# Last chunk of a Fourier mixing and gated feed-forward kernel: output product straight from h, in output rows

## The chip, the core and the metric

The kernel runs on one core of a Trainium2 chip. Five engines work side by side, each through its own list of instructions in order: TensorE (PE; its weight loads are shown as PEld), VectorE (DVE), ScalarE (ACT), GpSimd (POOL) and SyncE (SP), which here only issues transfers. ACT issues some transfers too. The metric is the time of one execution in microseconds (us) on the device.

## The reference

```python
batch, seq, dim = (8, 3008, 256)          # x, float32
X = np.fft.fft(x, axis=1)
X = np.fft.fft(X, axis=2)
x = X.real.astype(np.float32).reshape(24064, 256)
gate = 1.0 / (1.0 + np.exp(-(x @ w_gate)))   # w_gate, w_val: (256, 1536)
val = x @ w_val
out = (gate * val @ w_out).astype(np.float32)   # w_out: (1536, 256)
```

The three weight matrices come as float64; the kernel gets them as pairs of 32-bit words and converts them to float32 itself.

## The kernel before

**Staging.** The transform along the sequence uses the symmetry of cosine and sine: frequency k and its mirror image S − k come from the same two sums, kept for each batch element in tiles `pk` and `qk`, with the model dimension on partitions. The transform along the model dimension is multiplied into the gate and value weights once, at the start (`G1`, `G2`). So the feed-forward part begins with products of `G1` with `pk` and of `G2` with `qk`; their sum and their difference are the values of a frequency and of its mirror image.

**The main loop.** A batch element has 1505 frequencies, cut into six chunks: five of 252 columns and one of 246. Each chunk runs over 12 blocks `f` of 128 hidden features. That gives 8 x 6 x 12 = 576 iterations `i` of one loop (`count`), which is written out in order by hand (line 854): every engine's instructions stand in the order of the Python calls, and semaphores are put in from the tiles' use. An iteration has, in this order:

- `front_a(i)`: two products `pf<-pk,G` on PE into an accumulator bank (PSUM).
- `gate_a(i-1)`: ACT's sigmoid `h<-pf` (L627), and DVE's `z<-ae,pf` (L632), the other side's values.
- `part(i)`: ACT copies twice the `pk` part to `ae` (L608). The next products into that bank wait for it.
- `seed(i+1)`: two ACT instructions (L592) fill the next bank with one frequency's row.
- `gate_b(i-1)`: DVE's product L644, ACT's sigmoid L645 `z<-z`, DVE's product L646 `h<-z`; then POOL's sums `sf` (L650).
- `back`: five output products `po` for the group of features that was finished some iterations earlier.
- `front_b(i)`: two products `pf<-qk,G`.
- some entries of the list `later`, and whatever the table `side` holds for this iteration, at its end.

**The output product.** `h` holds, for 128 hidden features on partitions, both sides of the chunk: 2n columns. The 12 blocks go in four groups of three (`g`). Instead of 18 products of 128x128 blocks with a third of the columns each, a group needs 15, of sums of `h` blocks (`H_SUMS`, made on POOL) with sums of output-weight blocks (`wf`, made once at the start by `forms`). They accumulate over the four groups in five banks `po0` to `po4`. `back(p, part)` makes five products of group `p` in each of three iterations; for the last group of a chunk it also copies the banks to a tile `c` (ACT or DVE, L674). `finish` then needs 20 sums (`C_SUMS`, `C_LAST`; DVE, L697), four 32x32 block transposes (`flip`, L707), since the products lie with output features on partitions, and 16 stores (`store`, L716 and L720). For all chunks but the last these are put into `later`, two or three to an iteration (three in the last eight), so the chunk before last has its sums, transposes and stores inside the last chunk's iterations. For the last chunk they run at once; there POOL takes some of the sums, ACT issues half of the stores, and the last bank is read where it is.

**Tiles with one slot.** The pool `op` has a single slot for the tile `os` that takes the transposes; a new `os` waits for the transfers that read the one before. The pool `xp` has a single slot `x4` for the input of a batch element; the last one is read at iteration 472.

**Weights.** `weight_load` loads 256x256 float64 words (512 KB) on SP; `weight_parts` are two ACT instructions (L295, L296), `weight_join` three on DVE (L305, L306, L308) and an integer addition on POOL (L310). Before the change all weights pass through these in the first ten iterations or ahead of the loop, and only the sums of output weights in `wf` are kept.

Of the kernel before, what the change touches and what calls it, by code (L numbers as in the profile page):

```python
# [7 lines left out]
F32 = mybir.dt.float32  # L8
I32 = mybir.dt.int32
U32 = mybir.dt.uint32  # L10
AF = mybir.ActivationFunctionType
ALU = mybir.AluOpType
# [55 lines left out]
PLACE = (0, 1, 2, 5, 3, 4, 6, 7, 8, 9, 10, 11, 14, 13, 12)  # L68


C_SUMS = (((3, 3, 1, 0), 0), ((3, 3, 0, 1), 0), ((8, 1, 8, 0), 0), ((1, 6, 2, 0), 1), ((0, 0, 10, 1), 0),
          ((11, 0, 11, 0), 0), ((9, 9, 8, 0), 1), ((11, 11, 5, 0), 0), ((4, 4, 0, 1), 1),
          ((6, 11, 6, 0), 0), ((4, 4, 1, 0), 1), ((9, 13, 9, 1), 0), ((10, 14, 8, 1), 0), ((9, 9, 2, 0), 0),
          ((12, 9, 12, 0), 0), ((12, 12, 11, 1), 0), ((13, 13, 6, 1), 0),
          ((7, 7, 10, 0), 1), ((5, 5, 7, 1), 1))
C_LAST = (14, 9, 14, 0)
OUT = (3, 12)
HUGE = float((2 ** 24 - 1 - 2 ** 20) * 2.0 ** -7)
# [3 lines left out]
def kernel(  # L82
# [10 lines left out]
    nc = tc.nc  # L93
    B, _, _, _, D = xf.shape
    F = moe_w_gate.shape[1]
    P = 128
    S = out.shape[0] // B
    M = S // 2
    NK = M + 1
    NE = (M // 2) // 2 + 1  # L100
    NO = (M // 2) // 2
    NFT = F // P
    NPR = NFT // 2
    NG = NFT // 3
    CH = 252
    NB = 1 + max(b // 3 for b in PLACE)
# [26 lines left out]
    def mm(o, l, r, start, stop):  # L133
        nc.tensor.matmul(o, l, r, start=start, stop=stop, skip_group_check=True)  # L134
# [155 lines left out]
    def weight_parts(j):  # L290

        if j in RAW:
            raw, ws = RAW[j], WS[j]
            lo, hi = raw[:, :, :, 0], raw[:, :, :, 1]
            nc.scalar.activation(ws, hi.bitcast(F32), AF.Abs)  # L295
            nc.scalar.activation(lo, lo.bitcast(U32), AF.Copy, scale=2.0 ** -29)  # L296

    def weight_join(j):
        if j not in RAW:
            return  # L300
        raw, ws = RAW.pop(j), WS[j]
        lo, hi = raw[:, :, :, 0], raw[:, :, :, 1]
        wi = ws.bitcast(I32)
        ts = nc.vector.tensor_scalar
        ts(out=ws, in0=ws, scalar1=2.0 ** -15, scalar2=HUGE, op0=ALU.max, op1=ALU.min)  # L305
        ts(out=wi, in0=wi, scalar1=3, scalar2=0x3FFFFFF8, op0=ALU.logical_shift_left,  # L306
           op1=ALU.bitwise_and)
        nc.vector.scalar_tensor_tensor(out=wi, in0=hi, scalar=-(2 ** 30), in1=wi,  # L308
                                       op0=ALU.bitwise_and, op1=ALU.bitwise_or)
        nc.gpsimd.tensor_tensor(wi, wi, lo, op=ALU.add)  # L310

    WO, parts_ = {}, []

    def weight_use(j, other=None):
        w, c = jobs[j]
# [299 lines left out]
    def front_b(i):  # L615
        (_, qk, *_), ks, _, _, fs = cut(i)
        for g in range(2):
            mm(PF[i][:, g], G2[:, g, fs], qk[:, ks], False, True)
# [20 lines left out]
    def gate_b(i):  # L639

        n = cut(i)[2]
        p, fh = i // 3, i % 3
        z, h = Z.pop(i), H[p]
        nc.vector.tensor_tensor(h[:, fh, 0:n], h[:, fh, 0:n], PF.pop(i)[:, 1], op=ALU.mult)  # L644
        nc.scalar.activation(z[:, 0], z[:, 0], AF.Sigmoid)  # L645
        nc.vector.tensor_tensor(h[:, fh, n:], z[:, 0], z[:, 1], op=ALU.mult)  # L646
        if fh == 1:
            SF[p] = sp.tile([P, 8, 2 * CH // 3], F32, name="sf", tag="sf")
        for dst, a, b, op in H_SUMS.get(fh, ()):
            nc.gpsimd.tensor_tensor(block(p, dst), block(p, a), block(p, b),  # L650
                                    op=(ALU.subtract, ALU.add)[op])

    PO = []
    later = []
    C = {}

    def back(p, part):

        b, c, g = groups[p]
        n = chunks[c][1]  # L660
        R = 2 * n // 3
        last = p == len(groups) - 1
        if part == 0 and g == 0:
            PO[:] = [pso.tile([P, 2 * WC], F32, name=f"po{t}", tag=f"po{t}") for t in range(NB)]
        for at_, (hb, wb) in list(enumerate(PRODUCTS))[part * 5 : part * 5 + 5]:
            t, j = divmod(PLACE[at_], 3)
            mm(PO[t][:, j * R : (j + 1) * R], wf[:, g, wb], block(p, hb), g == 0 and at_ % 3 == 0,
               g == NG - 1)
            if g == NG - 1 and at_ % 3 == 2:
                if t == 0:  # L670
                    C[0] = cp.tile([P, 10 * WC], F32, name="c", tag="c")
                    nc.gpsimd.memset(C[0][:, 15 * R : 15 * R + 40], 0.0)
                if not (last and t == NB - 1):
                    (nc.vector.tensor_copy if t == 1 or t == 3 and not last else nc.scalar.copy)(  # L674
                        C[0][:, 3 * t * R : 3 * (t + 1) * R], PO[t][:, 0 : 3 * R])
        if part == 2:
            del H[p], SF[p]
            if g == NG - 1:
                finish(b, c, last)

    def finish(b, c, last):
        k0, n = chunks[c]
        R = 2 * n // 3
        more = k0 + n > NK
        nb = -(-n // TB)
        t = C.pop(0)
        queues = (nc.sync, nc.scalar) if last else (nc.sync,)
        os_ = []

        new = set()  # L690

        def sum_(dst, a, b, op, engine=nc.vector):

            there = lambda i: last and i >= 3 * (NB - 1) and i not in new
            v = [PO[NB - 1][:, (i - 3 * NB + 3) * R : (i - 3 * NB + 4) * R] if there(i) else
                 t[:, i * R : (i + 1) * R] for i in (a, b)]
            engine.tensor_tensor(t[:, dst * R : (dst + 1) * R], *v, op=(ALU.subtract, ALU.add)[op])  # L697
            new.add(dst)

        def flip(s, h):  # L700
            if not os_:

                full = (sp.tile([P, 8 * (2 * CH // 3)], F32, name="os", tag="sf") if last else
                        op.tile([P, NK + 1], F32, name="os", tag="os"))
                os_.append(full[:, 0 : 4 * WC].rearrange("p (s b h j) -> p s b h j", s=2, h=2, j=TB))
            c0 = OUT[h] * R + (n + more if s else 0)
            nc.vector.transpose(os_[0][:, s, 0:nb, h, :], t[:, c0 : c0 + nb * TB])  # L707

        def store(s):
            m, r0 = (min(n, M - k0), b * S + k0) if s == 0 else (  # L710
                n - (k0 == 0) - more, b * S + S - k0 - n + 1 + more)
            full = m // TB
            for a in range(4):
                ps = slice(a * TB, (a + 1) * TB)
                cs = slice(a * 2 * TB, (a + 1) * 2 * TB)
                queues[a % len(queues)].dma_start(  # L716
                    out=out[r0 : r0 + full * TB, cs].rearrange("(b t) d -> t b d", t=TB),
                    in_=os_[0][ps, s, 0:full].rearrange("p b h j -> p b (h j)"))
                if m > full * TB:
                    queues[a % len(queues)].dma_start(out=out[r0 + full * TB : r0 + m, cs],  # L720
                                      in_=os_[0][a * TB : a * TB + m - full * TB, s, full].rearrange(
                                          "p h j -> p (h j)"))

        def add(f):
            if last:
                f()
            else:
                later.append(f)
        for x, e in C_SUMS:
            if x[0] == 7:  # L730
                add(lambda: flip(0, 0))
                add(lambda: (flip(0, 1), store(0)))
            add(lambda x=x, e=e: sum_(*x, engine=(nc.vector, nc.gpsimd)[last and e]))
        add(lambda: sum_(*C_LAST))
        add(lambda: flip(1, 1))
        add(lambda: (flip(1, 0), store(1)))


# [61 lines left out]
    def at(i, *fs):  # L800
        side.setdefault(i, []).extend(fs)
# [29 lines left out]
    for b in range(B - 1):  # L831
# [17 lines left out]
        if b < B - 2:  # L849
            at(g0 + 1, lambda b=b: load_x(b + 2))  # L850
            for i, f in zip(calm(s0 if b else 3 * i0), mirror_x(b + 2)):
                at(i, f)

    for i in range(count):
        front_a(i)
        if N1 <= i < NFT:
            part(i)
        if i:
            gate_a(i - 1)
        if not N1 <= i < NFT:  # L860
            part(i)
        if i0 <= i + 1 < count:
            seed(i + 1)
        if i:
            gate_b(i - 1)
        todo = pre.pop(i, []) + use.pop(i, [])
        for f in [parts_.pop(0)] + todo if parts_ else todo + [lambda: parts_ and parts_.pop(0)()]:
            f()
        if i >= 5:
            back((i - 5) // 3, (i - 5) % 3)  # L870
        front_b(i)
        n = 3 if i >= count - 8 else 2 + i % 2
        for f in later[0:n]:
            f()
        del later[0:n]
        for f in side.pop(i, []):
            f()
    gate_a(count - 1)
    gate_b(count - 1)
    for f in later:  # L880
        f()
    for i in range(count, count + 5):
        back((i - 5) // 3, (i - 5) % 3)


# [47 lines left out]
```

## Time and profile before

| what | us |
| --- | --- |
| median of 3 runs | 1958.39 |
| lowest, highest run | 1955.29, 1959.18 |
| profiled execution: span from first to last instruction | 1957.5 |
| PE busy | 1915.8 (98%) |
| DVE, ACT, POOL busy | 1600.5, 1334.1, 1645.6 |
| granted TensorE clock, mean | 0.995 of full speed |

The page gives no other time of the profiled execution than its span; what the device spends around the first and the last instruction isn't in it. The span lies inside the range of the three runs.

How to read the rows: in the groups, "out<-in" are the program's tile names with partitions x elements; "xN" is the number of instructions; then busy time, mean duration, and the idle time of the engine ahead of them with what ended it. A float32 product appears as two weight loads and two matrix multiplications, so five products are ten records. In rows in order of time the first number is the start from the span's beginning, the second the duration, and the bracket the idle time ahead and its releaser. PE's rows end when the result is written, so successive ones overlap; the chain of waits counts each from where the one before it ended.

### The profile page before, as it was taken

Reading aid. Unit: us, or ns where it says so; the run is one execution under the profiler, and the core shown is the slowest. Engines: PE = TensorE matmul, PEld = TensorE weight load, DVE = VectorE, ACT = ScalarE, POOL = GpSimd, SP = SyncE. Lnnn points to the kernel's source line nnn. Section 1 sums busy time; section 2 is a strip of 40 time slices with the busy share of each in tenths; the row PEclk is TensorE's granted clock in tenths of the full one; section 3 lists DMA queues with packets and bytes.
Section 4 is the critical chain, followed back from the end, with each engine's and each line's share of the span. In section 5 each row is a group of like instructions: output and inputs, shape, how many; then the busy total and the mean of one; then the engine's idle time right before and its main releaser. Section 6 shows DMA issues by size and latency. Waiting matters only on the chain.

```text
span 1957.5 us, 34550 instructions
## 1 busy us (share of the span) xinstructions
PE 1915.8 (98%) x11252; PEld 1788.6 (91%) x11252; DVE 1600.5 (82%) x3271; ACT 1334.1 (68%) x3122; POOL 1645.6 (84%) x2853
## 2 busy tenths in 40 slices
PE   5999999999999999999999999999999999999997
PEld 3889899999999999999999999999999999999997
DVE  6888797898888878888878888788888887777777
ACT  2567667666777767776777767777677776777775
POOL 3779898997999978997889978998799996777776
PEclk9999999999999999999999999999999999999999
DMA  8352423212012120222012021211210110011011
GB/s 269 90 134 23 99 47 111 46 19 84 17 47 53 21 78 15 55 51 73 21 23 77 20 79 23 44 53 20 82 19 14 20 22 14 14 21 20 14 19 28
DMA packets 169746, 96.78 MB, mean 49 GB/s; under 512 B 133858, under 2 KB 161636, under 8 KB 167020
## 3 DMA queue, kind: packets, MB, share of 16 engines
q1 hardware_dynamic: 167596, 94.02, 20.2%
q8 instruction: 90, 1.47, 0.3%
q10 hardware_dynamic: 1940, 0.56, 0.2%
q14 instruction: 88, 0.72, 0.1%
q0 software_dynamic: 32, 0.00, 0.0%
HBM read 69.83 MB, written 46.71 MB: 60 GB/s over the span
## 4 chain that ended last, share of the span: by engine, by line
PE 90%; POOL 4%; DVE 3%; DMA 2%; ACT 1%; issue 0%; ACTq 0%; DVEq 0%; SPq 0%; POOLq 0%
PE pf L134 47%; PE po L134 39%; PE ev L134 2%; POOL sf L650 2%; DVE c L697 1%; DMA st<-in_stab_dram 1%; PE od L134 1%; PE ps L134 1%; DMA ge<-G 1%; DVE h L646 1%; DVE z L632 0%; ACT z L645 0%; POOL x L401 0%; DMA raw<-in_moe_w_gate_dram 0%; POOL x L417 0%
## 5 line engine op out<-in xcount | busy, mean ns | idle before, releaser
L650 POOL TENSOR_TENSOR sf<-h 128x168 f32<-128x168 f32 (+1 forms) x960 | 551.0, 593 | 196.9 <-DVE h L646 196.8
L650 POOL TENSOR_TENSOR sf<-h,sf 128x168 f32<-128x168 f32 (+1 forms) x1152 | 663.4, 595 | 46.7 <-DVE h L646 46.7
L134 PE MATMUL pf<-qk,G 128*128 128x252 f32 (+1 forms) x2304 | 583.0, 376 | 7.8 <-ACT ae L608 5.7
L134 PE MATMUL pf<-pk,G 128*128 128x252 f32 (+1 forms) x2304 | 583.7, 376 | 0.0
L646 DVE TENSOR_TENSOR h<-z 128x252 f32<-128x252 f32 (+1 forms) x576 | 316.5, 549 | 296.8 <-ACT z L645 294.9
L592 ACT ACTIVATE pf<-ek,ge 128x252 f32<-128x252 f32 (+1 forms) x1128 | 531.7, 471 | 18.4
L134 PE MATMUL po<-sf,wf 128*128 128x168 f32 (+1 forms) x3072 | 530.8, 306 | 0.2
L697 DVE TENSOR_TENSOR c<-c 128x168 f32<-128x168 f32 (+1 forms) x949 | 512.4, 571 | 5.5 <-ACT c L674 0.3
L134 PEld LDWEIGHTS pf<-pk,G 128*128 128x128 f32 x2304 | 436.3, 190 | 53.5 <-issue 1.6
L608 ACT ACTIVATE ae<-pf 128x504 f32<-128x504 f32 (+1 forms) x569 | 335.3, 589 | 216.1 <-PE pf L134 214.7
L134 PEld LDWEIGHTS po<-sf,wf 128*128 128x128 f32 x3072 | 473.3, 190 | 9.2 <-POOL sf L650 0.9
L134 PE MATMUL po<-h,wf 128*128 128x168 f32 (+1 forms) x2688 | 476.3, 306 | 0.0
L134 PEld LDWEIGHTS po<-h,wf 128*128 128x128 f32 x2688 | 428.1, 190 | 16.8
L134 PEld LDWEIGHTS pf<-qk,G 128*128 128x128 f32 x2304 | 409.8, 190 | 35.5 <-ACT ae L608 7.4
L632 DVE TENSOR_TENSOR z<-ae,pf 128x504 f32<-128x504 f32 (+1 forms) x569 | 377.7, 664 | 15.6 <-ACT h L627 15.2
L645 ACT ACTIVATE z<-z 128x252 f32<-128x252 f32 (+1 forms) x576 | 232.6, 404 | 161.5 <-DVE z L632 139.9
L627 ACT ACTIVATE h<-pf 128x252 f32<-128x252 f32 (+1 forms) x576 | 217.0, 377 | 125.9 <-PE pf L134 113.4
L644 DVE TENSOR_TENSOR h<-h,pf 128x252 f32<-128x252 f32 (+1 forms) x576 | 232.2, 403 | 0.0
L650 POOL TENSOR_TENSOR sf<-sf 128x168 f32<-128x168 f32 (+1 forms) x192 | 111.5, 581 | 15.1
L650 POOL TENSOR_TENSOR sf<-sf,h 128x168 f32<-128x168 f32 (+1 forms) x192 | 109.3, 569 | 0.0
L134 PE MATMUL ev<-st,x 63*128 63x189 f32 (+3 forms) x372 | 73.3, 347 | 11.5 <-DVE x L398 9.0
L674 ACT COPY c<-po 128x504 f32<-128x504 f32 (+1 forms) x144 | 80.2, 557 | 3.1 <-PE po L134 3.1
(138 smaller groups left out, 880.1 us busy)
## 6 DMA issues: line engine op xcount, KB each, us to landing
x<-xr SPq DMA_DIRECT2D x14, 1536.0 KB
out_dram<-os SPq DMA_DIRECT2D x380, 56.0 KB
xr<-in_xf_dram SPq DMA_DIRECT2D x14, 768.0 KB
xr<-in_xf_dram SPq DMA_DIRECT2D x35, 256.0 KB
ek<-ed SPq DMA_DIRECT2D x39, 126.0 KB
out_dram<-os SPq DMA_DIRECT2D x288, 7.0 KB
st<-in_stab_dram SPq DMA_DIRECT2D x4, 1111.9 KB
x<-in_xf_dram SPq DMA_DIRECT2D x2, 1512.0 KB
```

What stands on the lines that cost most here:

```text
L134: nc.tensor.matmul(o, l, r, start=start, stop=stop, skip_group_check=True)
L592: nc.scalar.activation(PF[i][:, g], EK[i // NFT], AF.Copy, scale=ge[:, g, f : f + 1])
L608: nc.scalar.activation(AP[i], PF[i], AF.Copy, scale=2.0)
L627: nc.scalar.activation(H[p][:, fh, 0:n], PF[i][:, 0], AF.Sigmoid)
L632: nc.vector.tensor_tensor(z[:, :, ::-1], AP.pop(i), PF[i], op=ALU.subtract)
L644: nc.vector.tensor_tensor(h[:, fh, 0:n], h[:, fh, 0:n], PF.pop(i)[:, 1], op=ALU.mult)
L645: nc.scalar.activation(z[:, 0], z[:, 0], AF.Sigmoid)
L646: nc.vector.tensor_tensor(h[:, fh, n:], z[:, 0], z[:, 1], op=ALU.mult)
L650: nc.gpsimd.tensor_tensor(block(p, dst), block(p, a), block(p, b), op=(ALU.subtract, ALU.add)[op])
L674: (nc.vector.tensor_copy if t == 1 or t == 3 and not last else nc.scalar.copy)(C[0][:, 3 * t * R : 3 * (t + 1) * R], PO[t][:, 0 : 3 * R])
L697: engine.tensor_tensor(t[:, dst * R : (dst + 1) * R], *v, op=(ALU.subtract, ALU.add)[op])
```

## The change

The last chunk (`p >= P_LAST`, the last four groups) doesn't use the sums:

- `gate_b` ends after `h` there: no `sf`, no POOL sums.
- Instead of `back`, a new function `straight(f)` multiplies one feature block of `h`, as the stationary operand, by 128 rows of the plain output weights. Its result has tokens on partitions, 256 output features in the columns, as the output has them. There are four row tiles (128, 116, 128 and 117 tokens: two for each side), two to a bank, so four products of 256 columns for each `f`, 48 in all. After the last `f` each tile is copied to `od` (DVE for tiles 0 and 2, ACT for 1 and 3) and stored by one transfer (SP and ACT). `od` is taken from the slot of `os`.
- The table `STRAIGHT` says which `f` is made in which of the last seven iterations; three are left for after the loop.
- The plain output weights aren't there any more, so `late_weights` loads them again, in six loads, into the slot `x4`: at iteration `count - 48 + 4c`, with `weight_parts` two iterations later and `weight_join` three iterations later, at the end of the iteration.
- `C_SUMS` loses its engine marks, and `back` and `finish` their cases for the last chunk.

```diff
+    def late_weights(c):
+        if not WL:
+            WL[0] = xp.tile([P, 24, WC], F32, name="wl", tag="x4")
+        ws = WL[0][:, 2 * c : 2 * c + 2]
+        src = moe_w_out[2 * c * P : 2 * (c + 1) * P, :].rearrange("(c p) f -> p c f", p=P)
...
+            r = 12 + c % 3 * 4
+            raw = WL[0][:, r : r + 4].rearrange("p a n -> p (a n)")
+            RAW[j] = raw.bitcast(I32).rearrange("p (c f w) -> p c f w", c=2, w=2)
+            nc.sync.dma_start(out=RAW[j].rearrange("p c f w -> p c (f w)"), in_=src.bitcast(I32))
...
         nc.vector.tensor_tensor(h[:, fh, n:], z[:, 0], z[:, 1], op=ALU.mult)
+        if p >= P_LAST:
+            return
...
+    def straight(f):
+        if not PD:
+            PD.extend(pso.tile([P, 2 * WC], F32, name=f"pd{t}", tag=f"po{t}") for t in range(2))
+            OD.append(op.tile([P, NK + 1], F32, name="od", tag="os")[:, 0 : 4 * WC].rearrange(
+                "p (t d) -> p t d", d=WC))
+        h = H[P_LAST + f // 3]
+        for t, (c0, m, row) in enumerate(tiles()):
+            o = PD[t // 2][0:m, t % 2 * WC : (t % 2 + 1) * WC]
+            mm(o, h[:, f % 3, c0 : c0 + m], WL[0][:, f], f == 0 and t % 2 == 0, f == NFT - 1)
+            if f == NFT - 1:
+                (nc.scalar.copy if t % 2 else nc.vector.tensor_copy)(OD[0][0:m, t], o)
+                (nc.scalar if t % 2 else nc.sync).dma_start(out=out[row : row + m, :], in_=OD[0][0:m, t])
...
+    for c in range(NPR):
+        i = count - 4 * i0 + 4 * c
+        at(i, lambda c=c: late_weights(c))
+        at(i + 2, lambda c=c: weight_parts(len(jobs) + c))
+        at(i + 3, lambda c=c: weight_join(len(jobs) + c))
+    STRAIGHT = {count - 7: (0, 1), count - 6: (2, 3), count - 5: (4,), count - 4: (5,), count - 3: (6,),
+                count - 2: (7,), count - 1: (8,), count: (9, 10, 11)}
...
-        if i >= 5:
+        if 5 <= i < 3 * P_LAST + 5:
             back((i - 5) // 3, (i - 5) % 3)
+        for f in STRAIGHT.pop(i, ()):
+            straight(f)
...
     for f in later:
         f()
-    for i in range(count, count + 5):
-        back((i - 5) // 3, (i - 5) % 3)
+    for f in STRAIGHT.pop(count):
+        straight(f)
```

## The prediction

> **What bounds the kernel now.** I read the page's first part, the waits of the last 150 us, the instructions in order of time for one ordinary iteration, for a stalled one and for the end, and then the rows of the weight conversion.
>
> ```profile
> PE 1915.8 (98%) x11252; PEld 1788.6 (91%) x11252; DVE 1600.5 (82%) x3271; ACT 1334.1 (68%) x3122; POOL 1645.6 (84%) x2853
> ```
>
> TensorE is the bound. In the waits from 1800 to 1935 us nobody makes PE wait: DVE waits for ACT, ACT for PE.
>
> ```profile
> POOL sf L650 <- DVE h L646: 32.1, 30, 2.0
> DVE h L646 <- ACT z L645: 29.6, 43, 1.3
> ACT ae L608 <- PE pf L134: 19.5, 44, 0.5
> ```
>
> Near there an iteration recurs every 3.125 us (252 columns), 3.05 us in the last chunk (246). One of them, in order of time (start, us, engine, what):
>
> ```profile
> 1815.50 1.85 DVE L697 TENSOR_TENSOR c<-c 128x168 f32<-128x168 f32 x3
> 1816.37 0.59 ACT L608 ACTIVATE ae<-pf 128x504 f32<-128x504 f32 x1 [0.47 <-PE pf L134]
> 1817.27 0.67 DVE L632 TENSOR_TENSOR z<-ae,pf 128x504 f32<-128x504 f32 x1
> 1817.46 0.76 PEld L134 LDWEIGHTS pf<-qk,G 128*128 128x128 f32 x4
> 1817.96 0.41 ACT L645 ACTIVATE z<-z 128x252 f32<-128x252 f32 x1
> ```
>
> PE needs ae, which ends 0.50 us ahead of its next pf products. ACT's L645 waits for DVE's z and stands ahead of the next ae, so a late DVE can reach PE. At 373 us it did:
>
> ```profile
> 372.89 0.59 ACT L608 ACTIVATE ae<-pf 128x504 f32<-128x504 f32 x1 [0.47 <-PE pf L134]
> 373.39 3.30 DVE L697 TENSOR_TENSOR c<-c 128x168 f32<-128x168 f32 x3
> 376.61 0.67 DVE L632 TENSOR_TENSOR z<-ae,pf 128x504 f32<-128x504 f32 x1
> 378.53 1.12 PE L134 MATMUL pf<-qk,G 128*128 128x252 f32 x4 [1.12 <-ACT ae L608]
> ```
>
> Three sums took 3.30 us beside large POOL work, z began 3.72 us after ae began, and that iteration of PE lasted 4.515 us, 1.4 too long. So z may begin 2.3 us after ae for nothing. Ordinarily DVE is free for its sums 0.87 us before ae (1815.50 against 1816.37): up to 3.17 us of work on DVE there is free.
>
> The end:
>
> ```profile
> 1939.94 0.77 DVE L707 STREAM_TRANSPOSE os<-c 128x256 f32<-128x256 f32 x2
> 1944.36 0.42 SPq L720 DMA_DIRECT2D out_dram<-os  x1
> 1944.62 2.11 PE L134 MATMUL po<-sf,wf 128*128 128x164 f32 x14
> 1946.53 2.25 DVE L697 TENSOR_TENSOR c<-c 128x164 f32<-128x164 f32 x4 [0.30 <-ACT c L674]
> 1951.38 0.77 DVE L707 STREAM_TRANSPOSE os<-c 128x256 f32<-128x256 f32 x2
> 1955.16 0.28 SPq L720 DMA_DIRECT2D out_dram<-os  x1
> ```
>
> PE ends at 1946.73; sums, transposes and stores take 10.8 us more to the span's 1957.5. The last pf product ends at F = 1939.77 by the chain of waits; from F to the end are 17.7 us.
>
> **The change, part by part.** Removed in the last chunk: 52 POOL sums of 0.54 to 0.6 us (beside PE, worth nothing on the path except through DVE's freedom), five po copies, all sums and transposes after PE, 16 small stores on SP and ACT.
>
> *PE.* Sixty products of 164 columns become 48 of 256. The chain has five of 164 in 1.39 us and 984 columns of pf in 1.66: both 1.69 ns a column. So 0.278 us a product before, 0.433 after; 16.7 us become 20.8, plus 4.1. By the order of the instructions two iterations get eight products each (3.46 for 1.39: plus 2.07 twice) and five get four (1.73: plus 0.34), so F moves by 5.85. After it 12 products stay (5.2) where 25 were (6.96). Nothing waits for the new products' weights or for h, which is three iterations old; only the last three f follow F closely, and h of the last (2.4 us after F in the old trace, 1939.77 to 1942.15) is ready before the 3.46 us of the two ahead of it are done.
>
> *The last row tiles.* In the changed order the copy of tile 0 from the accumulator (DVE) waits for eight DMA semaphores: `od` has the slot of the chunk before's `os`, whose stores must have landed. The second matmul into each bank waits for that bank's first copy, because the copy is written ahead of it. Tile 0 is multiplied at F + 9 x 0.433 = 3.9. The old stores end with the issue at 1944.36, F + 4.6, and land 1.45 later: F + 6.0. In the new run DVE makes the transposes some 0.8 us earlier against F (a longer iteration, no POOL sums), but SP still issues 16 stores at about 0.43 each, so I take half, F + 5.55. Then: DVE copy 0.43 (0.67 for 492 columns, L674, with 0.16 fixed); hand-over 0.06; matmul of tile 1 to its result 0.74 (0.58 for 164 columns at 1922.27, plus 92 x 1.69 ns); tile 2 0.43; its copy 0.48; tile 3 with hand-over 0.80; ACT copy 0.42; issue 0.05; landing 1.9 (1.2 to 1.8 for the last old stores by the trace's semaphore records; more bytes here); 1.1 from the last landing to the end, as before. F + 12.0. With F 5.85 later that is 17.8 against 17.7: plus 0.1. Bounds: without the store wait tile 0's copy starts at F + 4.1, 1.45 earlier (minus 1.3 in all); a landing like that of the ek load, 2.9, gives plus 1.1. I stay at the step's own sum, since the eight semaphores stand in the order.
>
> One rule concerns the stores. The Trainium skill, DMA: Bandwidth & Descriptors, in Why a DMA increments its semaphore by 16 and not by 1, says a copy from SP or ACT is spread over the largest number of engines up to 16 that divides its rows: 4 engines for the 116 rows of tile 1, 13 for the 117 of tile 3. No run here has such a store; if tile 1's became the last to land, the end would move beyond this sum.
>
> *Late weights.* Six times, four iterations apart from iteration 528: a 512 KB load on SP; two iterations later two ACT passes; one later three DVE passes and a POOL add.
>
> ```profile
> L295 ACT ACTIVATE wx<-wx x8: 664/670/679, 56.2 to 97.0; 128x512 f32<-128x512 f32 x8
> L305 DVE TENSOR_SCALAR wx<-wx x8: 412/716/764, 61.2 to 102.6; 128x512 f32<-128x512 f32 x8
> L306 DVE TENSOR_SCALAR wx<-wx x8: 427/646/1401, 61.6 to 103.4; 128x512 int32<-128x512 int32 x8
> L308 DVE SCALAR_TENSOR_TENSOR wx<-wx x8: 693/910/1664, 62.1 to 104.1; 128x512 int32<-128x512 int32 x8
> ```
>
> Loads: the wx loads landed 3.8 us after issue, the use is 6.2 after: hidden. On SP each stands ahead of eight stores and the next ek load, needed eight iterations later: hidden, unless SP is held over 20 us.
>
> ACT: 2 x 0.67 = 1.34 us behind L645 and ahead of the next ae. In the ordinary iteration ACT idles 0.5 and 0.47 there, so ae is 0.4 late; it has 0.5 less a 0.06 hand-over: nothing. In iterations 530 and 542 a 0.56 copy of po stands there too: ae is 0.9 late, PE loses some 0.35, twice: 0.7.
>
> DVE: 1.54 us by the shortest rows, 2.27 by the medians, 4.1 by the longest; the long ones lay beside POOL work. After the chunk's other DVE work: iterations 531, 543 have a copy (0.68), 535, 547 three sums (1.16, POOL mostly idle there), 539, 551 two transposes and a sum (1.4) beside POOL's sums. With 2.27 the three are 2.95, 3.43 and 3.67 against 3.17; in 535 and 547, where POOL idles, I take 1.54: 2.7. So only 539 and 551 stall, 0.5 each: 1.0. Lower end nothing (1.54 everywhere: 2.2, 2.7, 2.9); upper end, 4.1 six times: 1.6, 2.1 and 2.3, twice, 12 us. I take the median, as POOL is busy about three quarters of this stretch.
>
> POOL: 1.29 us more (L310) in 12.5, which adds a tenth to 77% busy; its sums are read two iterations later: hidden.
>
> A rule speaks against the change here. The row first: c sums take 0.33 us alone and about 0.6 beside POOL's, so POOL costs each about half of one of its own instructions. The Trainium skill, SBUF — State Buffer, SBUF: two separate sides, says the port pair of VectorE and GpSimd is an exclusive lock, and the loser is blocked for a whole instruction. By the rule each of the three passes waits one POOL sum and the join takes 3.3 us, and the whole change costs 8 us instead of 2.
>
> *Sum.* 4.1 of PE is inside the tail's plus 0.1; ACT 0.7; DVE 1.0: plus 1.8 us. The profiled execution is its span of 1957.5 us, 0.9 under the median of 1958.39 and inside the three runs; I add to the median: **1960.2 us**. About 0.2%, 3.9 us, is what a measurement of this kernel can tell from no change.
>
> **The rivals.** *Slower: the joins starve the gates.* If POOL stretches the three DVE passes everywhere, z comes late six times and PE stops behind L645. Halfway between the median and the longest rows, at 3.2 us, the excess over 3.17 is 0.7, 1.2 and 1.4, twice: 6.6, and with 0.8 from the rest 7.4: 1965.8. It leaves the band of no change where the join's mean passes 2.6 us. For it: 373 us, and L306 and L308 at twice their shortest time. Against it: those lie beside 128x512 POOL folds, which this stretch no longer has.
>
> *A small gain.* The store wait does not bind and the conversions hide: minus 1.3, 1957.1. For it: ACT and DVE idle a fifth of the stretch. Against it: SP's 0.43 us issues are regular.
>
> *Faster by over 0.2%.* Even without bank waits (12 products 5.2, result 0.3, copy 0.42, issue 0.05, landing 1.9, end 1.1: F + 9.0) the tail saves 2.9 us, so this needs an error in the PE step too.
>
> **How the numbers follow.** Forecast 0.46, small gain 0.08, starving 0.40, faster 0.06. Same is 0.54. The range goes from a gain of about 2 us, 1956.4, to past the starving case, 1966.5; the forecast's own is 1958 to 1962.3.
>
> **What would show it.** Right: pd products 0.43 us apart, PE gaps only near iterations 530, 539, 542, 551, of 0.3 to 0.5 us; F 5.85 plus those gaps later; the first od copy released by a DMA, some 1.5 us after tile 0's product; 12 us from F to the end. Wrong: PE gaps of 1 us at every join; wl landing after its use; a last store that lands 3 us after issue; pd products over 0.45 us.

## The result

The changed kernel takes 1962.97 us (median of 22 runs, 1959.35 to 1967.47), the kernel before 1956.63 in the same comparison (22 runs, 1953.96 to 1964.57): a ratio of 1.0031, 95% interval 1.0024 to 1.0038. It is about 6.1 us slower, more than the 0.2% that can be told from no change. The forecast was a loss of 1.8 us, within that band. 1962.97 lies in the whole range that was given and the direction holds, but it is above the forecast's own 1958 to 1962.3, and the loss is over three times the forecast: by that band of 0.2% the outcome is the slower one, which had a chance of 0.40 against the forecast's 0.46.

The profiled execution of the changed kernel took 1961.92 us, its span is 1960.1. Against the span of before that is only 2.6 us more, since the profiled run of before lost time at its start: the main loop's iteration 1 began at 58.02 us there and at 54.23 here, while the other profiles of this study have 53.3 to 55.4. From that iteration to the end the changed kernel needs 6.4 us more, which fits the ratio.

**Where they are.** I took the start of the first `pf` product of every iteration from the trace. Iterations are 3.125 us apart where nothing stalls.

| stretch | before | predicted | after |
| --- | --- | --- | --- |
| iterations 531 to 556, the six conversions: stalls | 0 | 1.7 | 6.1 |
| start of iteration 564 to that of 575: the new products in the loop | 33.74 | 39.20 | 39.20 |
| start of iteration 575 to the end | 20.93 | 15.57 | 15.95 |

The second row has the growth of 5.46 us that belongs to iterations before 575 (569 and 570 with 2.06 each, 571 to 574 with 0.335); the rest of the 5.85 is in iteration 575. Products and tail together cost 0.5, where 0.1 was forecast. So nearly the whole loss is in the late conversion of the weights. It isn't spread evenly: the four iterations 535, 539, 547 and 551 lose 0.93, 1.21, 0.93 and 1.18 us, and smaller losses lie beside them. Each of the four follows the one at whose end two ACT passes stand (534, 538, 546, 550).

**The profile after.** The page's first part:

```profile
PE 1923.4 (98%) x11228; PEld 1788.1 (91%) x11228; DVE 1606.4 (82%) x3272; ACT 1336.9 (68%) x3133; POOL 1625.3 (83%) x2800
```

Over the whole span no engine looks busier than before; DVE has 82% in both. The stretch tells more. The windows over the six conversions, first of the changed kernel, then of the kernel before (length, and busy time with number of instructions of PE, weight loads, DVE, ACT and POOL):

```profile
1793.00:1880.00 87.00, 83.64 (x468) 75.24 (x468) 74.35 (x150) 63.37 (x150) 72.61 (x120) 1.00 0.22 54
```

```profile
1797.00:1878.00 81.00, 81.00 (x468) 76.36 (x467) 59.58 (x133) 59.52 (x138) 60.93 (x115) 1.00 0.12 21
```

Both hold 468 records of PE, the same work, and the changed kernel needs 6 us more for it. DVE does 15 us more there and goes from 74% busy to 85%. The waits of that stretch (who waits for whom, us in all, times, longest), changed kernel:

```profile
ACT z L662 <- DVE z L649: 19.2, 16, 2.0
PEld pf L134 <- ACT ae L625: 5.3, 8, 1.2
PE pf L134 <- ACT ae L625: 3.1, 4, 0.9
```

None of these rows is there in the kernel before. Two of its own:

```profile
DVE h L646 <- ACT z L645: 19.9, 26, 1.3
ACT ae L608 <- PE pf L134: 11.7, 26, 0.5
```

(The lines have moved: L625, L649, L662, L663 and L735 are L608, L632, L645, L646 and L697 of before, and they move again from run to run; the tile names stay.) The order has turned round: ACT waits for DVE's `z` in 16 of some 27 iterations, and PE for ACT's `ae`. One of the large stalls, behind the ACT passes of iteration 538, in order of time:

```profile
1820.64 1.85 DVE L735 TENSOR_TENSOR c<-c 128x168 f32<-128x168 f32 x3
...
1822.42 0.67 DVE L649 TENSOR_TENSOR z<-ae,pf 128x504 f32<-128x504 f32 x1
...
1823.12 0.41 ACT L662 ACTIVATE z<-z 128x252 f32<-128x252 f32 x1 [1.41 <-DVE z L649]
...
1823.44 0.67 ACT L295 ACTIVATE wl<-wl 128x512 f32<-128x512 f32 x1
...
1824.00 0.67 ACT L296 ACTIVATE wl<-wl 128x512 int32<-128x512 uint32 x1
...
1824.82 0.60 ACT L625 ACTIVATE ae<-pf 128x504 f32<-128x504 f32 x1
...
1825.47 1.12 PE L134 MATMUL pf<-qk,G 128*128 128x252 f32 x4 [0.94 <-ACT ae L625]
```

DVE begins its three sums 0.39 us after the start of `ae` (1820.25), where in the iteration shown of before it began them 0.87 ahead. `z` then begins 2.17 us after `ae`, which by itself would cost nothing. But ACT has stood 1.41 us for it, and only then come the two passes, which the prediction had put into ACT's idle time. There is none left: the next `ae` is late, and PE waits 0.94 us. Why DVE is late is in the chain of waits, which leaves PE at iteration 535 and runs over DVE (start, us, what; the view leaves out its shortest pieces):

```profile
1815.46 0.69 DVE wl L308
1817.22 0.63 DVE h L663
1817.86 1.19 DVE c L735 x2
1820.72 1.20 DVE c L735 x2
1823.44 0.67 ACT wl L295
```

The first row is the join of the conversion before. Three iterations later the chain, still on DVE, meets the next conversion's ACT passes.

### The profile page after: what moved, and what is told of

It is laid out like the page before. It is cut to its first block, busy times and chain, and to the rows that moved or that the text cites. A ratio compares the mean times of both kernels' runs of the same rounds, so it can differ in the third digit from the quotient of the medians.

```text
span 1960.1 us, 34459 instructions
## 1 busy us (share of the span) xinstructions
PE 1923.4 (98%) x11228; PEld 1788.1 (91%) x11228; DVE 1606.4 (82%) x3272; ACT 1336.9 (68%) x3133; POOL 1625.3 (83%) x2800
## 4 chain that ended last, share of the span: by engine, by line
PE 87%; DVE 5%; POOL 3%; ACT 2%; DMA 2%; issue 1%; SPq 0%; ACTq 0%; DVEq 0%; POOLq 0%
PE pf L134 46%; PE po L134 37%; PE ev L134 2%; POOL sf L669 2%; DVE c L735 1%; DMA st<-in_stab_dram 1%; DVE h L663 1%; PE pd L134 1%; PE ps L134 1%; PE od L134 1%; DMA ge<-G 1%; DVE z L649 1%; ACT z L662 1%; POOL x L418 0%; ACT ae L625 0%
## 5 line engine op out<-in xcount | busy, mean ns | idle before, releaser
L669 POOL TENSOR_TENSOR sf<-h 128x168 f32<-128x168 f32 (+1 forms) x940 | 542.6, 597 | 182.2 <-DVE h L663 182.1
L669 POOL TENSOR_TENSOR sf<-h,sf 128x168 f32<-128x168 f32 (+1 forms) x1128 | 651.5, 597 | 43.7 <-DVE h L663 43.7
L663 DVE TENSOR_TENSOR h<-z 128x252 f32<-128x252 f32 (+1 forms) x576 | 318.8, 553 | 289.1 <-ACT z L662 287.4
L134 PE MATMUL po<-sf,wf 128*128 128x168 f32 (+1 forms) x3008 | 520.3, 306 | 0.2
L735 DVE TENSOR_TENSOR c<-c 128x168 f32<-128x168 f32 (+1 forms) x940 | 506.2, 570 | 4.9
L625 ACT ACTIVATE ae<-pf 128x504 f32<-128x504 f32 (+1 forms) x569 | 335.2, 589 | 209.7 <-PE pf L134 207.7
L134 PEld LDWEIGHTS po<-sf,wf 128*128 128x128 f32 x3008 | 463.7, 190 | 9.1 <-POOL sf L669 0.9
L134 PE MATMUL po<-h,wf 128*128 128x168 f32 (+1 forms) x2632 | 466.8, 306 | 0.0
L134 PEld LDWEIGHTS po<-h,wf 128*128 128x128 f32 x2632 | 419.5, 190 | 16.6
L649 DVE TENSOR_TENSOR z<-ae,pf 128x504 f32<-128x504 f32 (+1 forms) x569 | 377.7, 664 | 22.1 <-ACT h L644 21.7
L662 ACT ACTIVATE z<-z 128x252 f32<-128x252 f32 (+1 forms) x576 | 232.8, 404 | 178.6 <-DVE z L649 157.4
```

The costliest lines, as they stand in the source:

```text
L625: nc.scalar.activation(AP[i], PF[i], AF.Copy, scale=2.0)
L649: nc.vector.tensor_tensor(z[:, :, ::-1], AP.pop(i), PF[i], op=ALU.subtract)
L735: nc.vector.tensor_tensor(t[:, dst * R : (dst + 1) * R], *v, op=(ALU.subtract, ALU.add)[op])
```

## The experiments

Stalls are the sum of what the iterations from 476 to 563 took beyond the same iterations of the kernel before; the tail is from the start of iteration 575 to the end (before: 20.93). Both are counted in one profiled execution of each kernel. Each ratio is to the kernel before on the same chip. Unless said, an edit is to the changed kernel.

| kernel | ratio, 95% | stalls | tail |
| --- | --- | --- | --- |
| changed kernel | 1.0031 (1.0024 to 1.0038) | 6.1 | 15.95 |
| loads only | 0.9993 (0.9979 to 1.0008) | 0 | 15.21 |
| ACT passes only | 0.9993 (0.9983 to 1.0003) | 0 | 15.11 |
| join only | 1.0017 (1.0007 to 1.0027) | 3.1 | 16.56 |
| every twelfth iteration | 0.9995 (0.9984 to 1.0006) | 0 | 15.15 |
| every eighth iteration | 1.0009 (0.9998 to 1.0019) | 2.6 | 16.73 |
| one DVE pass to an iteration | 1.0023 (1.0014 to 1.0032) | 5.8 | 14.92 |
| no POOL addition | 1.0026 (1.0015 to 1.0036) | 5.3 | 15.77 |
| twelfth, own slot for `od` | 1.0002 (0.9993 to 1.0011) | 0 | 15.73 |
| the same, four banks | 0.9999 (0.9990 to 1.0007) | 0 | 14.99 |
| the same, all stores on SP | 0.9991 (0.9981 to 1.0001) | 0 | 13.12 |

### Which part of the conversion costs

Loads only:

```diff
+        nc.gpsimd.memset(ws, 0.01)
...
-        at(i + 2, lambda c=c: weight_parts(len(jobs) + c))
-        at(i + 3, lambda c=c: weight_join(len(jobs) + c))
```

> The changed kernel with the six loads but without the conversion: the two ACT passes, the three DVE passes and the POOL addition are left out, and the last chunk is multiplied by a constant instead of the output weights. Theory (the conversion costs the 6.1 us of PE gaps between iterations 530 and 556): every iteration there lasts 3.125 us again, F to the end stays 12 us, and the time is that of the kernel before plus 0 to 1 us. Rival (the loads, or the new end, cost it): gaps stay, or the time stays 5 to 7 us above before.

ACT passes only:

```diff
-        at(i + 3, lambda c=c: weight_join(len(jobs) + c))
```

> Only the two ACT passes of each conversion are kept; the three DVE passes and the POOL addition are left out, so the weights of the last chunk are not the right ones. Theory (DVE's lateness after a join and the next ACT passes, three iterations later, add up): ACT alone loses little, 0 to 0.8 us of PE gaps in all. Rival (the 1.34 us of ACT ahead of ae is too long by itself): 4 us or more, with the gaps of 0.9 and 1.2 us behind the passes of the second, third, fifth and sixth conversion as in the changed kernel.

Join only:

```diff
-        nc.gpsimd.tensor_tensor(wi, wi, lo, op=ALU.add)
+        if j < len(jobs):
+            nc.gpsimd.tensor_tensor(wi, wi, lo, op=ALU.add)
+        else:
+            nc.gpsimd.tensor_tensor(wi, wi, wi, op=ALU.subtract)
...
+        nc.gpsimd.memset(ws, 0.01)
...
-        at(i + 2, lambda c=c: weight_parts(len(jobs) + c))
```

> Only the three DVE passes and a POOL instruction of each conversion are kept, on a constant, and the POOL instruction subtracts the tile from itself; the ACT passes are left out, so the weights of the last chunk are zero. Theory (both add up): DVE runs late behind each join and ACT's second sigmoid waits for it, but PE loses only 0.7 to 2.5 us in all, at the joins. Rival (the joins starve the gates by themselves): 5 to 6 us of gaps stay.

Measured: 1956.24, 1956.00 and 1959.46 us, the kernel before 1956.25. The loads cost nothing. The ACT passes alone cost nothing either, at all six places, and that includes iterations 530 and 542, where the prediction had 0.35 each. The joins alone cost 3.1 us, three times the 1.0 of the prediction, above the 0.7 to 2.5 of this run's theory and below the 5 to 6 of its rival. The waits of the stretch with the joins alone:

```profile
ACT z L666 <- DVE z L653: 19.7, 16, 2.7
PEld pf L134 <- ACT ae L629: 2.8, 4, 1.2
```

ACT waits for DVE's `z` as often and as long as in the changed kernel; that is the joins' doing. PE waits for `ae` four times and not eight. So 0 and 3.1 make 6.1 together: the passes cost 3 us, but only on an ACT that DVE's lateness has already robbed of its idle time. The stalls of the joins alone have places: 1.17 us at iterations 541 and 553, two after the joins in 539 and 551, at 537 and 549 0.18 and 0.35, at 545 0.13, and after the first join nothing. The first of the two large ones:

```profile
1824.58 0.59 ACT L629 ACTIVATE ae<-pf 128x504 f32<-128x504 f32 x1
...
1828.08 0.67 DVE L653 TENSOR_TENSOR z<-ae,pf 128x504 f32<-128x504 f32 x1
```

`z` begins 3.50 us after `ae`. The prediction had 2.3 for nothing; the 1.20 over it is the stall of 1.17.

### How far apart they must be

```diff
-        i = count - 4 * i0 + 4 * c
+        i = count - 92 + 12 * c
```

> The conversions stand twelve iterations apart instead of four, from iteration 484; ACT passes two and DVE passes three iterations behind the load as before, all at the place in the chunk that the second conversion had (its passes were followed by a gap of 0.93 us). Theory (lateness left by the conversion before): no gap of 0.9 behind the ACT passes, 0 to 0.4 us a conversion, 0 to 2.4 us in all, time 0.5 to 3 us above before. Rival (each conversion costs about 1 us wherever it stands): six times 0.9 to 1.2, the time 6 us above before.

Measured: 1955.54 us, no stall at all, with the same instructions, where the theory had 0.5 to 3 us above the kernel before. But all six joins then stand at the eighth iteration of a chunk, so spacing and place aren't told apart. Every eighth iteration does that:

```diff
-        i = count - 4 * i0 + 4 * c
+        i = count - 84 + 8 * c
```

> The changed kernel with the six conversions every eighth iteration from 492 on instead of every fourth from 528 on; tail unchanged. Theory (DVE's lateness from one join is carried to the next conversion's ACT passes; with DVE 74 per cent busy in an ordinary iteration, eight iterations leave it 6.4 us of idle time for 2.3 to 3 us of join): gaps 0 to 1.0 us in all, none behind the ACT passes; time equal to the kernel before, ratio 0.999 to 1.0005. Rival (the place in the chunk decides: passes at the seventh and eleventh iteration of a chunk, which had the gaps of about 1 us, cost that wherever they stand): four of the six lie there, gaps of about 4 us, ratio 1.002.

Measured: 1958.8 us against 1956.46, stalls of 2.6 us: above the theory, under the rival, and neither had their places. Nearly all lie behind joins, and they depend on where in a chunk the join is. The joins in 503 and 527 (last iteration of a chunk) are followed by 0.8 and 0.6 us, those in 495 and 519 (fourth) by 0.5 and 0.4, those in 511 and 535 (eighth) by nothing. Behind ACT passes there is one, of 0.2 us in iteration 519, where ACT also waited 0.17 for the load. So the place alone explains why every twelfth iteration cost nothing; whether the distance had a part there isn't shown. The joins eight apart and four apart stand at the same three places of a chunk, two at each. With conversions eight apart these places cost 2.6 us; crowding them adds the other 3.5.

The stall behind the join in 503 shows how a single one goes:

```profile
1711.59 0.42 DVE L663 TENSOR_TENSOR h<-z 128x246 f32<-128x246 f32 x1 [0.39 <-ACT z L662]
1711.96 0.77 DVE L743 STREAM_TRANSPOSE os<-c 128x256 f32<-128x256 f32 x2
...
1712.43 0.59 ACT L625 ACTIVATE ae<-pf 128x504 f32<-128x504 f32 x1 [0.50 <-PE pf L134]
...
1715.51 0.65 DVE L649 TENSOR_TENSOR z<-ae,pf 128x492 f32<-128x492 f32 x1
...
1717.40 1.12 PE L134 MATMUL pf<-qk,G 128*128 128x252 f32 x4 [0.52 <-ACT ae L625]
```

Transposes, a sum and the join are 3.55 us. DVE was free for them only 0.47 us ahead of `ae`, not 0.87, because ACT's passes one iteration earlier had made the last `h` late. So `z` begins 3.08 us after `ae`; 2.3 was for nothing, and the 0.78 that is over is the stall of 0.79.

### Burst or load, and the part of POOL

One DVE pass in each of three iterations, four iterations apart as in the changed kernel:

```diff
-        at(i + 3, lambda c=c: weight_join(len(jobs) + c))
+        at(i + 3, lambda c=c: weight_join(len(jobs) + c, (0,)))
+        at(i + 4, lambda c=c: weight_join(len(jobs) + c, (1,)))
+        at(i + 5, lambda c=c: weight_join(len(jobs) + c, (2,)))
```

> The changed kernel with the conversions four iterations apart, but the three DVE passes in three successive iterations, one in each, instead of all in one. If it is the burst of 1.5 to 2.3 us that makes DVE late, the gaps go: 0 to 1.5 us in all. If it is DVE's load over the whole stretch (85% busy in the changed kernel against 74% before), lateness is the same on average and 3 to 6 us stay.

No addition on POOL for the late weights:

```diff
-        nc.gpsimd.tensor_tensor(wi, wi, lo, op=ALU.add)
+        if j < len(jobs):
+            nc.gpsimd.tensor_tensor(wi, wi, lo, op=ALU.add)
```

> The changed kernel without the POOL addition of each late conversion (1.29 us of POOL, six times), so that the weights lack their low words and the result is a little less exact. If DVE's own three passes make it late, 4 to 6.1 us of gaps stay. If it is POOL's long instruction that holds DVE's sums and products up, as at 373 us in the kernel before, less than 3 us stay.

Measured: 1961.67 and 1961.82 us, the kernel before 1956.67. Breaking the burst up gives back next to nothing (stalls of 1.08, 1.24, 0.75, 1.35 and 1.27 at 535, 539, 543, 547 and 551, each one iteration behind ACT passes). DVE then never has more than one pass, 1.03 us at the longest, in an iteration, so a long join isn't needed for the loss. The run isn't a clean test of the burst, though: its third pass stands one iteration ahead of the next conversion's ACT passes instead of three, and the three passes took 2.5 us together. It fits that what counts is how much DVE has to do over the stretch and that the next passes come before it has caught up. Without POOL's six additions of 1.29 us, 7.7 us in all, the stalls are 0.8 less.

### The tail

The changed tail has three things in a row behind the last products. Its chain of waits:

```profile
1951.19 1.45 DMA out_dram<-os
...
1952.71 0.40 issue
1953.11 0.43 DVE od L697
...
1953.59 1.37 PE pd L134 x4
...
1954.98 0.44 DVE od L697
...
1955.46 1.22 PE pd L134 x2
...
1956.70 0.37 ACT od L697
```

The last old store lands, DVE's first copy starts, tiles 1 and 3 are multiplied only after the copy of the other tile in their bank. To see what each wait is worth, three kernels take them away one after the other, with the conversions every twelfth iteration so that nothing else disturbs.

A slot of its own for `od`:

```diff
-            OD.append(op.tile([P, NK + 1], F32, name="od", tag="os")[:, 0 : 4 * WC].rearrange(
+            OD.append(sp.tile([P, 8, 2 * CH // 3], F32, name="od", tag="sf").rearrange("p a b -> p (a b)")[:, 0 : 4 * WC].rearrange(
```

> Conversions twelve iterations apart, as in the run before (no PE gaps there), and od in a slot of its own, so that its copies wait for no old store. Theory (the copy of row tile 0 waits for the stores of the chunk before): the first copy starts right behind its product, 1.3 to 2.5 us earlier, and the end comes 1 to 2 us earlier after the last loop iteration than in the run before (15.2 us): 13.2 to 14.2. Rival (the stores have landed anyway): 15 to 16 us still.

Measured: 1956.90 us, tail 15.73, the rival's number for another reason. The wait went, and the time didn't:

```profile
1948.10 0.42 DVE L697 COPY od<-pd 128x256 f32<-128x256 f32 x1 [1.92 <-PE pd L134]
...
1949.70 0.27 ACTq L698 DMA_DIRECT2D out_dram<-od  x1
...
1952.55 0.33 SPq L756 DMA_DIRECT2D out_dram<-os  x1
1952.98 0.82 SPq L698 DMA_DIRECT2D out_dram<-od  x2
```

The first copy follows its product, as expected. But in the trace's records eight DMA semaphores go round over the transfers of both queues, and SP's sixteenth old store has the same one as the 116-row store that ACT had issued at 1949.70. It may not go before that has landed, 2.86 us after its issue, and the two `od` stores of SP stand behind it.

A bank for each row tile as well:

```diff
-            PD.extend(pso.tile([P, 2 * WC], F32, name=f"pd{t}", tag=f"po{t}") for t in range(2))
+            PD.extend(pso.tile([P, 2 * WC], F32, name=f"pd{t}", tag=f"po{t}") for t in range(4))
...
-            o = PD[t // 2][0:m, t % 2 * WC : (t % 2 + 1) * WC]
-            mm(o, h[:, f % 3, c0 : c0 + m], WL[0][:, f], f == 0 and t % 2 == 0, f == NFT - 1)
+            o = PD[t][0:m, 0:WC]
+            mm(o, h[:, f % 3, c0 : c0 + m], WL[0][:, f], f == 0, f == NFT - 1)
```

> As the run with od in its own slot, and each row tile in an accumulator bank of its own, so that no product waits for a copy of its bank. By the sum of the prediction for an end without these waits (F + 9.0 instead of F + 12.0) it ends some 3 us earlier than the changed kernel's end, about 12.3 us after the last loop iteration's start, and 2 to 4 us under the kernel before (0.1 to 0.2%). Rival (the waits were hidden behind the stores' landing): no gain over the run with od in its own slot.

Measured: 1955.84 us, tail 14.99 against some 12.3 expected. PE no longer waits, and the same wait of SP takes most of the gain; SP's waits from 1940 us to the end:

```profile
SPq L756 <- DMA out_dram<-od: 4.2, 1, 4.2
```

All four `od` stores on SP, so that no transfer of another queue comes between:

```diff
-                (nc.scalar if t % 2 else nc.sync).dma_start(out=out[row : row + m, :], in_=OD[0][0:m, t])
+                nc.sync.dma_start(out=out[row : row + m, :], in_=OD[0][0:m, t])
```

> The kernel of the run before this one of the tail (conversions every twelfth iteration, a slot of its own for od, a bank for each row tile), with all four od stores on SP, behind the 16 old stores. Theory (the shared DMA semaphores made SP's sixteenth old store wait for the landing of ACT's 116-row store, 2.86 us after its issue, and the od stores on SP stood behind it): that wait, 4.2 us, goes; the old stores end about 4.2 us earlier, the four od stores follow 0.43 us apart, the 116-row one lands 2.9 us after its issue, and the end after iteration 575's start falls from 15.0 us to 12.3 (12.0 to 12.8); 2.5 to 3 us under that kernel, a ratio to the kernel before of 0.998 to 0.999. Rival (SP's row of issues is what sets the end, the wait only lies in front of it): four issues more on SP cost what the wait gave, end at 14.5 to 15.5, ratio 1.000.

Measured: 1955.16 us against 1956.46, tail 13.12. The wait is gone and the tail 1.9 us shorter, not 2.7, between the ranges of theory and rival:

```profile
1947.98 0.43 SPq L756 DMA_DIRECT2D out_dram<-os  x1
1948.41 0.42 DVE L697 COPY od<-pd 128x256 f32<-128x256 f32 x1 [1.92 <-PE pd L134]
1948.85 0.37 ACT L697 COPY od<-pd 116x256 f32<-116x256 f32 x1 [2.80 <-PE pd L134]
1948.87 1.66 SPq L698 DMA_DIRECT2D out_dram<-od  x4
```

SP's row of stores ends just as the first copy begins, the four new ones take 1.66 us, and, close together, the last three land 2.7 to 2.9 us after their issue by the semaphore records, where the 117-row one took 1.9 when it was alone. From the last `pf` product to the end are 9.6 us, where the prediction's sum without these waits had 9.0. This kernel is the fastest of the study, but its interval reaches past 1: that it beats the kernel before isn't shown.

## Why the prediction was wrong in size

**Right.** The products: 1.73 us for four of them in the chain of waits, 0.433 each, and iterations 569 and 570 lose 2.06, 571 to 574 0.335, as worked out. The last row tiles: `od` waits for the landing of the old stores, the banks wait for their first copy, and products and tail together cost 0.5 where 0.1 was written; with loads only, with the ACT passes only and with conversions every twelfth iteration they gain 0.3. That the sum came so near is in part luck: the last old store landed 4.9 us after the last `pf` product, not 5.55, and the copy behind it began 0.40 late. The tolerance of 2.3 us between `ae` and `z` held too: `z` 3.08 and 3.50 us after `ae` cost 0.79 and 1.17. The loads land 3.7 to 6.6 us after their issue, ahead of their use. POOL's part is small. The rule of the Trainium skill, DMA: Bandwidth & Descriptors, on rows and engines: the 116-row store landed 2.86 us after its issue in the changed kernel, the 128-row ones 1.72 and 2.46, the 117-row one 1.88, which agrees with it, as do the semaphore records: after the issue 4 counts for the 116-row store and 13 for the 117-row one. The 116-row store wasn't the last to land, so it didn't set the end.

**Right place, wrong size: the joins.** "Only 539 and 551 stall, 0.5 each": alone they cost 1.17 each, and 0.8 and 0.6 in the same place with the conversions eight apart. The durations weren't at fault. In the changed kernel the three passes took 2.33 us in 539 and 551 (0.77, 0.65 and 0.91), 1.54 in 535 and 547 and 2.02 in 531 and 543, where 2.27, 1.54 and 2.27 were taken. What was over-estimated is the 3.17 us that were free. It was read from an ordinary iteration, in which DVE comes to its spare work 0.87 us ahead of `ae`; at the joins it came 0.47 ahead (503 above) or, four apart, behind it (0.29 behind at the join in 539 of the run with joins alone).

**Wrong: the step "ACT".** "`ae` is 0.4 late; it has 0.5 less a 0.06 hand-over: nothing" and "PE loses some 0.35, twice: 0.7". Alone the passes cost 0, so the first half held and the second was too high (by its own figures it is 0.46 each and not 0.35: 0.9 less the 0.44 that `ae` has). In the changed kernel the stalls of about 1 us, which the prediction had looked for at the joins if it was wrong, stand behind these passes. The step priced them on an ACT that waits for nobody; just ahead of the passes of 534 and 546 ACT had waited 0.88 us for `z`, of 538 and 550 1.41, and the 1.34 us came on top: 0.93 and 1.2 us of stall.

Behind both is one omission in "Late weights": each insertion was compared with the idle time of one undisturbed iteration, and the results were added. DVE is 74% busy there, so that it recovers about 0.8 us in an iteration, and four iterations give back 3.2 us at the most, by an estimate that lets it use all its idle time, to a join of 1.5 to 2.3. Lateness is handed on from one conversion to the next; the sum of the parts, 0 and 3.1, isn't the cost of both, 6.1. That the lateness passes over DVE is shown by the chain of waits and by the waits for `z`; that crowding makes 3.5 us of the loss, by the run with eight iterations between; how much of that is the passes' own and how much the joins delaying each other wasn't taken apart further.

**The rival "the joins starve the gates"** has the better number, 7.4 us for the change, and the right link (`z` late, PE stopped behind ACT's `z`), by another cause: it wanted joins of 3.2 us stretched by POOL, and they took 1.5 to 2.3. (By the rows shown there the longest passes add up to 3.83 us and not 4.1; that makes its joins 3.05 and its loss 6.6, and the joins' upper end 10 us and not 12.) The same goes for the rule of the Trainium skill, SBUF — State Buffer, on the one port pair, by which each pass waits for a whole POOL instruction and the change costs 8 us. (The page limits the lock to VectorE instructions with two SBUF inputs or in a two-port mode, a condition that the prediction left out.) The passes were to take 3.3 us by it; the longest joins took 2.33, and without POOL's addition 5.3 us of the 6.1 stay.

## What to carry to other kernels

Free time on an engine isn't a sum that each insertion can draw on: work out how late the engine will still be when the next insertion comes, and how much it recovers in between, before two insertions are priced as if alone. Where an insertion may be put anywhere, place and distance decide; here the same instructions cost 6.1, 2.6 or nothing. When a wait is taken away in a tail, look at what the queue beside it waits for, shared DMA semaphores among it.

## What the runs showed of the hardware

**PE's clock fell where PE had been idle for some 2 of 3.41 us.** In the tail PE waits for DVE's first copy. Where it had waited 1.60 to 1.91 us, the three products left took 1.12 us (two) and 0.69 (one). In the kernels where it waited 1.97 to 2.07, the last took 1.20 and in most of them the two before 1.36 to 2.03 also. The windows over these last products of the changed kernel and of the one with conversions every twelfth iteration, the granted clock being the third number from the end:

```profile
1952.69:1957.14 4.45, 2.56 (x6) 1.12 (x6) 0.85 (x2) 0.74 (x2) 0.00 (x0) 0.69 0.27 82
```

```profile
1947.54:1951.19 3.65, 1.81 (x6) 0.94 (x6) 0.85 (x2) 0.74 (x2) 0.00 (x0) 1.00 0.25 74
```

A clock of 0.69 against 1.00 is worth 0.75 us here (1.36 and 1.20 against 1.12 and 0.69), more than the 0.4 by which the tail missed its forecast; the tails of 15.8 to 16.7 us in the table that have `od` in the slot of `os` are those with the low clock, those of 14.9 to 15.2 have the full one. The wait itself is longer in the slow ones because the copy starts 0.40 us after DVE's semaphore wait ends, and 0.04 in the other kernel; why, these runs don't show. What went with the fall is how much of a fixed stretch PE is idle, more than how long one wait is. By the clock records of all twelve traces the granted clock is 1.00 or 0.50 and changes only at times that lie multiples of 3.41 us apart. It fell 40 times, each time at the end of a stretch of 3.41 us in which PE had been idle for 1.96 us or more; in the 6,737 other stretches at full clock PE was idle for 1.97 us at the most. In the changed kernel the fall came at 1954.34 us, between the products after the wait; in the kernel without POOL's addition one product later, so that two of the three still took 1.12. No run set out to try this, and another execution may meet the stretches otherwise. The Trainium skill, TensorE: Matmul & The Clock Gate, What's actually happening, gives an idle window of about 3.4 us before the clock falls; the length of the window agrees, but here some 2 us of idle PE within it were enough.

**DMA semaphores tie the queues together.** SP stood 4.2 us for a transfer that ACT had issued, with no data in common; with all four stores on SP it didn't.
